# First phase of an adaLN, attention and feed-forward kernel: one PSUM tile for the one-column products, one reading engine per PSUM tile, one more head computed in this phase, weight sums one per step

## The chip, the cores and the metric

The kernel runs on one core of one Trainium2 chip. The metric is the device time of one execution in microseconds (us). The profile's span, from the first to the last instruction, is about 1.7 us shorter than that time. Engines: PE is TensorE (matmuls), DVE is VectorE, ACT is ScalarE, SP only issues DMAs here. The record shows different chips for the later sets of runs (0, 1 and 14), so times are compared with the runs of before in the same set; profiles of different sets are compared across chips.

## The reference, cut to what matters

```python
mod = (silu(c) @ w_mod)            # six vectors of 1024: sa, ca, ga, sb, cb, gb
h = layernorm(x) * (1 + ca) + sa   # x: 2048 x 1024
q = h @ wq                         # 32 heads of 128; K and V: the last 512 rows of the caches
x = x + ga * (softmax(q k^T / sqrt(128)) v @ wo)
h = layernorm(x) * (1 + cb) + sb
x = x + gb * ((silu(h @ w_gate) * (h @ w_up)) @ w_down)
```

The kernel treats x in four chunks of 512 rows. In the first phase it makes the first chunk's normalized and transposed input and the q of the first heads while the weights are still coming in. As sa is known late, q is first computed from `hs = layernorm(x) * (1 + ca)`, and `sa @ wq` is added afterwards as a bias, one column per head (`bias_q`). Then come 128 steps (4 chunks x 32 heads) of scores, exponentials, q of the head seven steps ahead, the products with V, and output projections; then the feed-forward part.

Names in the profiles: xn are normalized rows, hT the transposed (and later modulated) input, wm and wq tiles of w_mod and wq, qT a head's q, s_ps the scores, pT their exponentials, o_ps the products with V, a_ps the output projection, guT the input of the last feed-forward product.

## The kernel before

The parts that the change and the argument touch. PSUM tiles of tag "mm" have four buffers of 512 FP32 columns each (called one bank below), those of tag "s" two buffers of two banks each.

```python
def mm(name, shape=(P, 512), dt=FP32):
    return psp.tile(list(shape), dt, name=name, tag="mm", bufs=4)
def big(name, shape=(P, 2, 512), dt=FP32):
    return psp.tile(list(shape), dt, name=name, tag="s", bufs=2)
# ... all DMA loads are issued from SP, in this order:
for tt in range(QT):
    load_x(tt)
for half in range(DH):
    load_wm(1, half); load_wq8(2 * half); load_wq8(2 * half + 1)   # ca; wq of heads 0..7
load_wm(0, 0); load_wm(0, 1)                                       # sa
# kT: 4 DMA transposes; v_sb: 4 loads
load_wq(0, 2)                                                      # wq of heads 8..11
# ...
h_scale(0, h0_ps[0][:, 0, :])               # DVE;  hs = h * (1 + ca), read from PSUM
mod_cols(1, 0, ca1, True, (1,))
h_scale(1, h0_ps[0][:, 1, :], True)         # ACT, the same PSUM tile
mod_cols(1, 0, ca1, True, (2, 3))
h_scale(2, h0_ps[0][:, 2, :])               # DVE
h_scale(3, h0_ps[0][:, 3, :], True)         # ACT
for dt in (0, 2):
    nc.vector.tensor_copy(out=h10[:, dt:dt + 2, :], in_=h0_ps[0][:, dt:dt + 2, :])
nc.scalar.copy(out=h10[:, 4:8, :], in_=h0_ps[1])
# ... q of heads 4..6 (tag "mm"), then 0..3 (tag "s", two heads in one tile)
for g in range(4):
    q0(g, range(4, DT))
sa_cols(0)                                  # 32 one-column matmuls, DVE copies to sa, sa_bf
q0(4, range(4, DT))
# ... modulation of h10 on DVE
shift_cols(0)                               # 28 one-column matmuls: sa @ wq, lower half
q0(5, range(4, DT))
sa_cols(1)
q0(6, range(4, DT))
shift_cols(1)                               # upper half, DVE adds: bias_q
for g in range(4):
    put_q(g, q0_ps[g], bias_q[:, g:g + 1], g % 2 == 1)   # odd heads on ACT
# ... rest of the modulation; put_q of 4..6; head 7 follows in step 0, between the first scores
```

Of the kernel before, what the change touches and what calls it, by code (L numbers as in the profile page):

```python
# [9 lines left out]
ALU = mybir.AluOpType  # L10
AX = mybir.AxisListType
BF16 = mybir.dt.bfloat16
# [576 lines left out]
def fast_path(ctx, tc, flag, A_x, A_k_cache, A_v_cache, A_wq, A_wo, B_x, B_w_gate, B_w_up,  # L589
# [3 lines left out]
    nc = tc.nc  # L593
    P = 128
    _, S, D = A_x.shape
    _, Hkv, Sk, Dh = A_k_cache.shape
    HD = A_wq.shape[1]
    H = HD // Dh
# [5 lines left out]
    NTC = S // TCW  # L604
    QT = TCW // P
    DT = D // P
# [28 lines left out]
    wk = ctx.enter_context(tc.tile_pool(name="work", bufs=2))  # L635
# [13 lines left out]
    def mm(name, shape=(P, 512), dt=FP32):  # L649
        return psp.tile(list(shape), dt, name=name, tag="mm", bufs=4)  # L650
# [19 lines left out]
    def chain(start):  # L670

        last = {}
        for ins in nc.cur_bb.bb.instructions[start:]:
            if ins.engine in last:
                tc.add_manual_dep(
                    ins, last[ins.engine],
                    mybir.DependencyInfo(mybir.DependencyClass.NoSync,
                                         mybir.DependencyReason.DATA), reason="chain")
            last[ins.engine] = ins.name
# [12 lines left out]
    wm_tiles = {}  # L692
# [14 lines left out]
    H0 = 7  # L707
# [14 lines left out]
    h10 = hpool.tile([P, DT, TCW], BF16, name="hT", tag="hT")  # L722
    load_wm(0, 1)
    kT = blkB("kT", [P, Hkv, W])
    for kv in range(Hkv):
        pin(nc.sync.dma_start_transpose(
            out=kT[:, kv, :], in_=A_k_cache[0, kv, k0:k0 + W, :]), "dma")
# [21 lines left out]
    sa, ca1, sb, cb1 = (modT[:, i, :] for i in range(4))  # L749
# [12 lines left out]
    siluc = const.tile([P, DT], BF16, name="siluc")  # L762
# [5 lines left out]
    def mod_cols(vec, half, dst, add_one, tiles=(0, 1, 2, 3)):  # L768
        wm = wm_tiles[(vec, half)]
        ps = mm("mod_ps", (P, 4))  # L770
        for i in tiles:
            for dt in range(DT):
                nc.tensor.matmul(ps[:, i:i + 1], lhsT=wm[:, dt, i * P:(i + 1) * P],  # L773
                                 rhs=siluc[:, dt:dt + 1], start=(dt == 0), stop=(dt == DT - 1))
        i0, i1 = tiles[0], tiles[-1] + 1
        nc.vector.tensor_scalar(out=dst[:, 4 * half + i0:4 * half + i1], in0=ps[:, i0:i1],
                                scalar1=1.0 if add_one else 0.0, scalar2=None, op0=ALU.add)
# [4 lines left out]
    c_bc = const.tile([P, D], BF16, name="c_bc")  # L782
# [40 lines left out]
    def at(k, f, *a):  # L823
        tasks.setdefault(k, []).append((f, a))
# [15 lines left out]
        nc.scalar.activation(out=mv[:, 2:3], in_=mv[:, 2:3], func=ACT.Exp, scale=-0.5)  # L840
        ln[tt] = mv

    def ln_norm(tt, on_act=False):
        mv = ln.pop(tt)
        n = wk.tile([P, D], BF16, name="xn", tag="xn", bufs=3)
        if on_act:
            nc.vector.scalar_tensor_tensor(out=mv[:, 3:4], in0=mv[:, 0:1], scalar=-1.0,
                                           in1=mv[:, 2:3], op0=ALU.mult, op1=ALU.mult)
            nc.scalar.activation(out=n, in_=xt[tt], func=ACT.Identity, bias=mv[:, 3:4],
                                 scale=mv[:, 2:3])  # L850
        else:
            pin(nc.vector.tensor_scalar(out=n, in0=xt[tt], scalar1=mv[:, 0:1],  # L852
                                        scalar2=mv[:, 2:3], op0=ALU.subtract, op1=ALU.mult))
        return n

    xn = {}

    def ln_rows(tt):
        xn[tt] = ln_norm(tt)

    def ln_xpose(key, tt):
        t = tt % QT
# [5 lines left out]
    def ln_affine(key, dt, ps, sc, sh, on_act):  # L868
        if on_act:
            nc.scalar.activation(out=hT[key][:, dt, :], in_=ps, func=ACT.Identity,  # L870
                                 bias=sh[:, dt:dt + 1], scale=sc[:, dt:dt + 1])
        else:
            pin(nc.vector.tensor_scalar(out=hT[key][:, dt, :], in0=ps, scalar1=sc[:, dt:dt + 1],
                                        scalar2=sh[:, dt:dt + 1], op0=ALU.mult, op1=ALU.add))

    def ln_mod(key, dt, sc, sh):
        ln_affine(key, dt, hT[key][:, dt, :], sc, sh, False)
# [27 lines left out]
    def plan_late_ln(k, key, sc, sh):  # L905

        for t in range(QT):
            tt = key[1] * QT + t
            at(k + 2 * t, late_stats, tt)
            at(k + 10 + 2 * t, ln_rows, tt)  # L910
            at(k + 11 + 2 * t, ln_xpose, key, tt)
        at(k + 8, late_rstd)
        for dt in range(DT):
            at(k + 24 + dt, ln_mod, key, dt, sc, sh)
# [13 lines left out]
    LEAD = H0  # L928
    qT = {}

    def put_q(g, q_ps, bias=None, on_act=False):
        t = wk.tile([P, TCW], BF16, name="qT", tag="row", bufs=LEAD + 2)
        if bias is None:
            nc.vector.tensor_copy(out=t, in_=q_ps)  # L934
        elif on_act:
            nc.scalar.activation(out=t, in_=q_ps, func=ACT.Identity, bias=bias)  # L936
        else:
            nc.vector.tensor_scalar(out=t, in0=q_ps, scalar1=bias, scalar2=None, op0=ALU.add)
        qT[g] = t
# [4 lines left out]
    h0_ps = [big("h0_ps", (P, 4, TCW), BF16) for _ in range(2)]  # L944
# [45 lines left out]
    hs = [blkA("hs", [P, 4, TCW]) for _ in range(DH)]  # L990

    def h_scale(dt, src=None, on_act=False):
        src = h10[:, dt, :] if src is None else src
        if on_act:
            nc.scalar.activation(out=hs[dt // 4][:, dt % 4, :], in_=src, func=ACT.Identity,  # L995
                                 scale=ca1[:, dt:dt + 1])
        else:
            nc.vector.tensor_scalar(out=hs[dt // 4][:, dt % 4, :], in0=src,
                                    scalar1=ca1[:, dt:dt + 1], scalar2=None, op0=ALU.mult)

    h_scale(0, h0_ps[0][:, 0, :])
    mod_cols(1, 0, ca1, True, (1,))
    h_scale(1, h0_ps[0][:, 1, :], True)
    mod_cols(1, 0, ca1, True, (2, 3))
    h_scale(2, h0_ps[0][:, 2, :])
    h_scale(3, h0_ps[0][:, 3, :], True)
    for dt in (0, 2):
        nc.vector.tensor_copy(out=h10[:, dt:dt + 2, :], in_=h0_ps[0][:, dt:dt + 2, :])
    nc.scalar.copy(out=h10[:, 4:8, :], in_=h0_ps[1])

    q0_mm = [mm("q_ps") for _ in range(H0 - 4)]
    q0_ps = {4 + i: t for i, t in enumerate(q0_mm)}

    def w0(g, dt):
        return wq8[dt // 2][:, dt % 2, g * P:(g + 1) * P]

    def q0(g, dts):
        for dt in dts:
            nc.tensor.matmul(q0_ps[g], lhsT=w0(g, dt), rhs=hs[dt // 4][:, dt % 4, :],  # L1019
                             start=(dt == 0), stop=(dt == DT - 1))  # L1020

    sa_bf = const.tile([P, DT], BF16, name="sa_bf")
    bias_q = const.tile([P, H0], FP32, name="bias_q")

    def shift_cols(half):
        ps = mm("sh_ps", (P, H0))
        for g in range(H0):
            for i in range(4):
                dt = 4 * half + i
                nc.tensor.matmul(ps[:, g:g + 1], lhsT=w0(g, dt), rhs=sa_bf[:, dt:dt + 1],  # L1030
                                 start=(i == 0), stop=(i == 3))
        if half == 0:
            nc.vector.tensor_copy(out=bias_q, in_=ps)
        else:
            nc.vector.tensor_tensor(out=bias_q, in0=ps, in1=bias_q, op=ALU.add)  # L1035

    def sa_cols(half):
        mod_cols(0, half, sa, False)
        nc.vector.tensor_copy(out=sa_bf[:, 4 * half:4 * half + 4],
                              in_=sa[:, 4 * half:4 * half + 4])  # L1040

    for dt in range(4):
        for g in range(4, H0):
# [1 line left out]
    for i in range(2):  # L1045
# [4 lines left out]
        if i == 0:  # L1050
            mod_cols(1, 1, ca1, True)
            for dt in range(4, DT):
                h_scale(dt)
    for g in range(4):
        q0(g, range(4, DT))
    sa_cols(0)
    q0(4, range(4, DT))
    for dt in range(4):
        ln_mod(("h1", 0), dt, ca1, sa)
    shift_cols(0)  # L1060
    q0(5, range(4, DT))
    sa_cols(1)
    q0(6, range(4, DT))
    shift_cols(1)
    for g in range(4):
        put_q(g, q0_ps[g], bias_q[:, g:g + 1], g % 2 == 1)
    for dt in range(4, DT):
        ln_mod(("h1", 0), dt, ca1, sa)
    for g in range(4, H0):
        put_q(g, q0_ps[g], bias_q[:, g:g + 1])  # L1070
    chain(first)

    k_ld = []
# [183 lines left out]
    for hg in range(H // 4):  # L1257
        for i in range(2):
            for j in range(2):
                at((1 + hg % (NTC - 1)) * H + max(0, 4 * hg - 3 + 2 * i + j), bound_wq, hg, i, j)  # L1260
    at(NU - H + 2, load_k)
    for kv in range(Hkv):
        at(NU - H + 20 + 2 * kv, bound_k, kv)
# [76 lines left out]
    for k in range(NU + 1):  # L1340
        if k % 4 >= 2 and 4 * (k // 4) + 12 < NU:
            g = 4 * (k // 4) + 12
            load_wq(g // H, (g % H) // 4, (k % 4 - 2,))
        if k < NU:
            emit_s(k)
        if k + LEAD < NU:
            emit_q(k + LEAD)
        if k == NU - 5:
            load_gu(0, 0)
        run_tasks(k)  # L1350
        if k >= 1:
            emit_o(k - 1)
# [76 lines left out]
```

## Time and profile before

| | before |
|---|---|
| time, median of 3 | 1273.99 us (1273.82 to 1274.0) |
| span of the profiled run | 1272.5 us |
| PE / DVE / ACT busy | 99% / 48% / 26% |
| first wide q matmul starts | 12.21 us |
| first o_ps group (product with V) starts | 35.11 us |
| stretch between these two | 22.90 us |

From the first o_ps group on, PE repeats a fixed pattern, so the stretch between the last two marks says how well the first phase runs. The page's busy line:

```profile
PE 1254.6 (99%) x7445; PEld 640.9 (50%) x7587; DVE 608.9 (48%) x1335; ACT 335.3 (26%) x440; POOL 1.3 (0%) x10
```

The timeline of PE in the kernel before, cut to the lines around its idle times. The columns are start, duration, engine, line, operation, output and inputs, shape and count; in brackets the idle time before the group and what ended it.

```profile
12.21 2.82 PE L1019 MATMUL q_ps<-hs,wq 128*128 128x512 bf16 x11
15.49 1.90 PE L1019 MATMUL q_ps<-hs,wq 128*128 128x512 bf16 x8 [0.47 <-DVE hT L1008]
...
29.20 1.02 PE L1148 MATMUL q_ps<-hT,wq 128*128 128x512 bf16 x4 [0.26 <-DVE bias_q L1035]
30.77 0.59 PE L1159 MATMUL s_ps<-qT,kT 128*128 128x512 bf16 x2 [0.54 <-ACT qT L936]
...
32.92 0.59 PE L1148 MATMUL q_ps<-hT,wq 128*128 128x512 bf16 x2
...
35.11 1.07 PE L1191 MATMUL o_ps<-v_sb,pT 128*128 128x130 bf16 x16
```

Wide matmuls follow each other every 0.216 us, and a group's printed duration includes the last one's tail. So the twelve q matmuls from 12.21 (one record of them is missing) need 2.6 us, and PE could have gone on at 14.8 or 14.9; it went on at 15.49. Counted in this way the three idle times are 0.6, 0.4 and 0.7 us. Head 7's eight matmuls are the four at 29.20 and two pairs, cut here, at 31.20 and 32.06.

Where the first of these comes from is seen in the timeline of ACT and DVE over the same microseconds:

```profile
12.19 0.69 ACT L995 ACTIVATE hs<-h_ps,modT 128x512 bf16<-128x512 bf16 x1 [2.06 <-DVE modT L776]
...
12.91 0.48 DVE L998 TENSOR_SCALAR hs<-h_ps,modT 128x512 bf16<-128x512 bf16 x1 [0.36 <-ACT hs L995]
...
13.43 0.69 ACT L995 ACTIVATE hs<-h_ps,modT 128x512 bf16<-128x512 bf16 x1 [0.55 <-DVE hs L998]
...
14.01 1.86 ACT L1009 COPY hT<-h_ps 128x2048 bf16<-128x2048 bf16 x1
14.15 1.29 DVE L1008 COPY hT<-h_ps 128x1024 bf16<-128x1024 bf16 x2 [0.75 <-ACT hs L995]
```

The two engines take turns on one PSUM tile, each waiting for the other. Only the ACT copy at 14.01 overlaps DVE, and it reads the other tile.

One more stall lies in step 32. The groups of o_ps are 5.22 us apart in this part. The timelines of PE and DVE near 180 us:

```profile
178.04 1.07 PE L1191 MATMUL o_ps<-v_sb,pT 128*128 128x130 bf16 x16
...
178.87 1.22 DVE L1082 SCALAR_TENSOR_TENSOR junk<-wq 128x1024 bf16<-128x1024 bf16 x1
...
180.12 1.23 DVE L1082 SCALAR_TENSOR_TENSOR junk<-wq 128x1024 bf16<-128x1024 bf16 x1
...
181.47 1.22 DVE L1082 SCALAR_TENSOR_TENSOR junk<-wq 128x1024 bf16<-128x1024 bf16 x1
...
182.95 1.22 DVE L1082 SCALAR_TENSOR_TENSOR junk<-wq 128x1024 bf16<-128x1024 bf16 x1
...
188.79 1.07 PE L1191 MATMUL o_ps<-v_sb,pT 128*128 128x130 bf16 x16
```

Four weight sums (they feed a bound on the scores) stand in one step, and two steps take 10.75 us instead of 10.45. All waits of PE in the list of waits (total, times, longest) are these:

```profile
PE h_ps L948 <- DVE xn L852: 2.3, 2, 2.1
PE warm_ps L746 <- DVE warm_w L737: 1.6, 1, 1.6
PE s_ps L1159 <- ACT qT L936: 0.5, 1, 0.5
PE q_ps L1019 <- DVE hT L1008: 0.5, 1, 0.5
PE gu_ps L1305 <- DVE guT L1311: 0.3, 1, 0.3
PE q_ps L1148 <- DVE bias_q L1035: 0.3, 1, 0.3
```

### The profile page before, as it was taken

What the parts mean: (1) busy time and instruction counts of PE and PEld (TensorE: products, weight loads), DVE (VectorE), ACT (ScalarE), POOL (GpSimd) and SP (SyncE); (2) the same over time, 40 slices, a digit from 0 to 9 for tenths busy, and PEclk for the clock granted to TensorE, in tenths of its full rate; (3) what the DMA queues carried; (4) which work ended last, traced back from release to release, by engine and by line L of the source; (5) the groups of instructions that cost most, each with busy time, mean ns of one, the idle gap of its engine ahead of it and who ended that gap; (6) DMA issues with size and microseconds to landing.
All of it is one profiled execution on the core that took longest, in us unless ns stands there. A gap on an engine that the chain in (4) does not pass through costs nothing.

```text
span 1272.5 us, 18029 instructions
## 1 busy us (share of the span) xinstructions
PE 1254.6 (99%) x7445; PEld 640.9 (50%) x7587; DVE 608.9 (48%) x1335; ACT 335.3 (26%) x440; POOL 1.3 (0%) x10
## 2 busy tenths in 40 slices
PE   8999999999999999999999999999999999999998
PEld 4555555555555555555554444444444444444444
DVE  4766568966587756476664632321122112221122
ACT  3643334443343333334341111011100111011100
POOL 0000000000000000000000000000000000000000
PEclk9999999999999999999999999999999999999999
DMA  9897658787656655454575479326633565425702
GB/s 291 197 246 182 178 128 174 174 172 193 144 137 171 154 137 153 113 154 115 117 202 146 132 224 252 95 92 209 211 113 111 167 207 188 157 91 168 246 17 69
DMA packets 306844, 204.46 MB, mean 161 GB/s; under 512 B 145601, under 2 KB 303297, under 8 KB 306754
## 3 DMA queue, kind: packets, MB, share of 16 engines
q1 hardware_dynamic: 301842, 199.03, 57.5%
q10 hardware_dynamic: 4912, 4.20, 1.0%
q8 instruction: 61, 1.00, 0.3%
q14 instruction: 29, 0.24, 0.1%
HBM read 165.94 MB, written 4.21 MB: 134 GB/s over the span
## 4 chain that ended last, share of the span: by engine, by line
PE 96%; DVE 1%; DMA 1%; issue 1%; ACT 0%; SPq 0%; DVEq 0%; ACTq 0%
PE gu_ps L1305 29%; PE a_ps L1223 17%; PE q_ps L1148 16%; PE d_ps L1325 15%; PE o_ps L1191 9%; PE s_ps L1159 8%; DMA hT<-xn 1%; PE q_ps L1019 1%; DMA x<-in_A_x_dram 0%; DVE junk L1082 0%; PE mod_ps L773 0%; DVE st L833 0%; DVE xn L852 0%; ACT hs L995 0%; PE sh_ps L1030 0%
## 5 line engine op out<-in xcount | busy, mean ns | idle before, releaser
L1161 ACT ACTIVATE pT<-s_ps 128x1024 bf16<-128x1024 f32 x256 | 249.1, 1020 | 347.0 <-PE s_ps L1159 234.5
L1223 PE MATMUL a_ps<-wo,oT 128*128 128x512 bf16 x989 | 240.1, 379 | 1.9
L1148 PE MATMUL q_ps<-hT,wq 128*128 128x512 bf16 x966 | 228.7, 379 | 0.3 <-DVE bias_q L1035 0.3
L1311 DVE TENSOR_TENSOR guT<-gu_ps,sg 128x512 bf16<-128x512 f32 x112 | 77.4, 691 | 284.1 <-ACT sg L1310 284.1
L1305 PE MATMUL gu_ps<-hT,wg 128*128 128x512 bf16 x875 | 209.8, 379 | 1.4 <-DVE guT L1311 0.3
L1310 ACT ACTIVATE sg<-gu_ps 128x512 bf16<-128x512 f32 x112 | 66.9, 597 | 489.1 <-PE gu_ps L1305 474.9
L1325 PE MATMUL d_ps<-wd,guT 128*128 128x512 bf16 (+2 forms) x934 | 193.2, 366 | 0.9
L1305 PE MATMUL gu_ps<-hT,wu 128*128 128x512 bf16 x659 | 162.0, 379 | 0.7
L1223 PEld LDWEIGHTS <-oT 128*128 128x128 bf16 x1024 | 100.1, 98 | 120.6
L934 DVE CAST qT<-q_ps 128x512 bf16<-128x512 f32 x121 | 83.5, 690 | 148.1 <-PE q_ps L1148 147.1
L1148 PEld LDWEIGHTS <-wq 128*128 128x128 bf16 x968 | 94.7, 98 | 114.2 <-issue 0.3
L1325 PEld LDWEIGHTS <-guT 128*128 128x128 bf16 x952 | 90.9, 98 | 103.0
L1191 PEld LDWEIGHTS <-pT 128*128 128x128 bf16 x2048 | 126.7, 98 | 30.8 <-issue 0.4
L1305 PEld LDWEIGHTS <-wg 128*128 128x128 bf16 x896 | 87.6, 98 | 106.0 <-issue 0.6
L1191 PE MATMUL o_ps<-v_sb,pT 128*128 128x130 bf16 x2048 | 137.1, 220 | 0.1
L1159 PE MATMUL s_ps<-qT,kT 128*128 128x512 bf16 x467 | 129.5, 379 | 2.9 <-ACT qT L936 0.5
L1305 PEld LDWEIGHTS <-wu 128*128 128x128 bf16 x672 | 65.7, 98 | 79.3
L1178 DVE TENSOR_TENSOR oq<-o_ps,rl 128x256 bf16<-128x256 f32 (+2 forms) x256 | 100.3, 418 | 3.7
L1329 DVE TENSOR_TENSOR f<-d_ps,gb_bc 128x512 f32<-128x512 f32 (+2 forms) x34 | 22.4, 660 | 140.8 <-PE d_ps L1325 140.8
L1231 DVE TENSOR_TENSOR acc<-a_ps,acc 128x512 f32<-128x512 f32 x64 | 44.0, 687 | 37.2 <-PE a_ps L1223 37.2
L1159 PEld LDWEIGHTS <-kT 128*128 128x128 bf16 x512 | 44.9, 98 | 31.3 <-issue 1.0
L1305 PE MATMUL gu_ps<-hT,v_sb 128*128 128x512 bf16 x220 | 57.0, 379 | 0.2
(92 smaller groups left out, 419.1 us busy)
## 6 DMA issues: line engine op xcount, KB each, us to landing
wq<-in_A_wq_dram SPq DMA_DIRECT2D x64, 512.0 KB
wo<-in_A_wo_dram SPq DMA_DIRECT2D x64, 512.0 KB
wg<-in_B_w_gate_dram SPq DMA_DIRECT2D x56, 512.0 KB
wd<-in_B_w_down_dram SPq DMA_DIRECT2D x56, 512.0 KB
wu<-in_B_w_up_dram SPq DMA_DIRECT2D x42, 512.0 KB
v_sb<-in_B_w_up_dram SPq DMA_DIRECT2D x14, 512.0 KB
x<-in_A_x_dram SPq DMA_DIRECT2D x16, 256.0 KB
wm<-in_w_mod_dram SPq DMA_DIRECT2D x4, 1024.0 KB
```

Source lines behind the costliest of these rows:

```text
L934: nc.vector.tensor_copy(out=t, in_=q_ps)
L1148: nc.tensor.matmul(q_ps, lhsT=w, rhs=hT[("h1", cc)][:, dt, :], start=(dt == 0), stop=(dt == DT - 1))
L1159: nc.tensor.matmul(s_ps[:, i, :], lhsT=kT[:, kv, j * P:(j + 1) * P], rhs=qT[g], start=True, stop=True)
L1161: nc.scalar.activation(out=p[:, 2 * jj:2 * jj + 2, :], in_=s_ps, func=ACT.Exp, scale=scale)
L1178: nc.vector.tensor_tensor(out=dst, in0=ps[:, s0:s0 + cnt, 0:Dh], in1=sc, op=ALU.mult)
L1191: nc.tensor.matmul(o_slot["ps"][:, s_, :], lhsT=pT[g][:, j, t * P:(t + 1) * P], rhs=v_sb[:, kv, j, 0:VN], start=(j == 0), stop=(j == WT - 1))
L1223: nc.tensor.matmul(a_ps, lhsT=oT[(cc, 2 * q + i)][:, hh % 4, t * P:(t + 1) * P], rhs=wo_tiles[(cc, q, dh, i)][:, hh % 4, :], start=(hh == ...
L1231: nc.vector.tensor_tensor(out=acc[(cc, t)][:, dsl], in0=a_ps, in1=acc[(cc, t)][:, dsl], op=ALU.add)
L1305: nc.tensor.matmul(ps[:, n, :], lhsT=gu_w[(cc, fg, nm, dt // 4)][:, dt % 4, fi * P:(fi + 1) * P], rhs=hT[("h2", cc)][:, dt, :], start=(dt ...
L1310: nc.scalar.activation(out=g, in_=ps[:, 0, :], func=ACT.Silu)
L1311: nc.vector.tensor_tensor(out=guT[(cc, fg)][:, fi, :], in0=ps[:, 1, :], in1=g, op=ALU.mult)
L1325: nc.tensor.matmul(d_ps, lhsT=guT[(cc, f // 4)][:, f % 4, t * P:(t + 1) * P], rhs=wd_tiles[(cc, dh, f // 4)][:, f % 4, c0:c0 + w], start=( ...
```

## The change

Its intent is to remove these idle times. (a) Each PSUM tile has one reading engine: DVE does all four scalings and the copies of h0_ps[0], ACT only copies h0_ps[1]; qT of heads 0 and 1 is written by DVE, of heads 2 and 3 by ACT. (b) The one-column products share one PSUM tile, are cut into pieces, and stand between pairs of wide matmuls. (c) Head 7 is computed in full in the first phase, behind the last one-column products, from the already modulated input h10. (d) The weight sums stand one per step, seven steps ahead of their group's heads; before, the first group's four stood in one step and the others one per step, three steps ahead. (e) The fourth normalized row of the last chunk uses the buffer c_bc, which is free by then.

```diff
-            at(k + 10 + 2 * t, ln_rows, tt)
+            at(k + 10 + 2 * t, ln_rows, tt, c_bc if t == QT - 1 else None)
...
     h_scale(0, h0_ps[0][:, 0, :])
+    nc.scalar.copy(out=h10[:, 4:8, :], in_=h0_ps[1])
     mod_cols(1, 0, ca1, True, (1,))
-    h_scale(1, h0_ps[0][:, 1, :], True)
+    h_scale(1, h0_ps[0][:, 1, :])
...
-    h_scale(3, h0_ps[0][:, 3, :], True)
+    h_scale(3, h0_ps[0][:, 3, :])
...
+    one_ps = mm("one_ps", (P, 3, 8))
...
-    for g in range(4):
+    for g in range(3):
         q0(g, range(4, DT))
-    sa_cols(0)
-    q0(4, range(4, DT))
+
+    q0(3, (4, 5))
+    sa_mm(0, (0, 1))
+    q0(3, (6, 7))
+    sa_mm(0, (2, 3))
+    sa_out(0)
+    q0(4, (4, 5))
+    sh_mm(0, range(4))
+    q0(4, (6, 7))
+    sh_mm(0, range(4, H0))
... # the same for the upper half, with heads 5 and 6
+    for dt in (4, 5):
+        ln_mod(("h1", 0), dt, ca1, sa)
+    for dt in (6, 7):
+        ln_affine(("h1", 0), dt, h10[:, dt, :], ca1, sa, True)
+    nc.vector.tensor_tensor(out=bias_q, in0=one_ps[:, 2, 0:H0], in1=bias_q, op=ALU.add)
+    q0_ps[H0] = mm("q_ps")
+    q0(H0, range(DT), h10)
     for g in range(4):
-        put_q(g, q0_ps[g], bias_q[:, g:g + 1], g % 2 == 1)
+        put_q(g, q0_ps[g], bias_q[:, g:g + 1], g >= 2)
...
-                at((1 + hg % (NTC - 1)) * H + max(0, 4 * hg - 3 + 2 * i + j), bound_wq, hg, i, j)
+                at((1 + hg % (NTC - 1)) * H + 4 * hg - LEAD + 2 * i + j, bound_wq, hg, i, j)
...
-        if k + LEAD < NU:
+        if 0 < k < NU - LEAD:
             emit_q(k + LEAD)
```

Here `sa_mm` makes column sums of sa, `sa_out` has DVE copy them to sa and sa_bf, and `sh_mm` multiplies sa_bf with wq. The last hunk: q of head 8 now follows directly after the first scores.

More of the change, by code (lines that the diff above doesn't have):

```diff
@@ L841, in ln_stats, with ln_norm @@
         ln[tt] = mv
-    def ln_norm(tt, on_act=False):
+    def ln_norm(tt, on_act=False, n=None):
         mv = ln.pop(tt)
-        n = wk.tile([P, D], BF16, name="xn", tag="xn", bufs=3)
+        n = wk.tile([P, D], BF16, name="xn", tag="xn", bufs=3) if n is None else n
         if on_act:
@@ L856, in fast_path, with ln_rows @@
     xn = {}
-    def ln_rows(tt):
-        xn[tt] = ln_norm(tt)
+    def ln_rows(tt, n=None):
+        xn[tt] = ln_norm(tt, n=n)
     def ln_xpose(key, tt):
@@ L1001, in fast_path, with q0 @@
     h_scale(0, h0_ps[0][:, 0, :])
+    nc.scalar.copy(out=h10[:, 4:8, :], in_=h0_ps[1])
     mod_cols(1, 0, ca1, True, (1,))
-    h_scale(1, h0_ps[0][:, 1, :], True)
+    h_scale(1, h0_ps[0][:, 1, :])
     mod_cols(1, 0, ca1, True, (2, 3))
     h_scale(2, h0_ps[0][:, 2, :])
-    h_scale(3, h0_ps[0][:, 3, :], True)
+    h_scale(3, h0_ps[0][:, 3, :])
     for dt in (0, 2):
         nc.vector.tensor_copy(out=h10[:, dt:dt + 2, :], in_=h0_ps[0][:, dt:dt + 2, :])
-    nc.scalar.copy(out=h10[:, 4:8, :], in_=h0_ps[1])
     q0_mm = [mm("q_ps") for _ in range(H0 - 4)]
     q0_ps = {4 + i: t for i, t in enumerate(q0_mm)}
+    one_ps = mm("one_ps", (P, 3, 8))
     def w0(g, dt):
         return wq8[dt // 2][:, dt % 2, g * P:(g + 1) * P]
-    def q0(g, dts):
+    def q0(g, dts, src=None):
         for dt in dts:
-            nc.tensor.matmul(q0_ps[g], lhsT=w0(g, dt), rhs=hs[dt // 4][:, dt % 4, :],
+            nc.tensor.matmul(q0_ps[g], lhsT=w0(g, dt),
+                             rhs=hs[dt // 4][:, dt % 4, :] if src is None else src[:, dt, :],
                              start=(dt == 0), stop=(dt == DT - 1))
@@ L1023, in fast_path, with sh_mm, sa_mm, sa_out @@
     bias_q = const.tile([P, H0], FP32, name="bias_q")
-    def shift_cols(half):
-        ps = mm("sh_ps", (P, H0))
-        for g in range(H0):
+    def sh_mm(half, heads):
+        for g in heads:
             for i in range(4):
                 dt = 4 * half + i
-                nc.tensor.matmul(ps[:, g:g + 1], lhsT=w0(g, dt), rhs=sa_bf[:, dt:dt + 1],
-                                 start=(i == 0), stop=(i == 3))
-        if half == 0:
-            nc.vector.tensor_copy(out=bias_q, in_=ps)
-        else:
-            nc.vector.tensor_tensor(out=bias_q, in0=ps, in1=bias_q, op=ALU.add)
-    def sa_cols(half):
-        mod_cols(0, half, sa, False)
-        nc.vector.tensor_copy(out=sa_bf[:, 4 * half:4 * half + 4],
-                              in_=sa[:, 4 * half:4 * half + 4])
+                nc.tensor.matmul(one_ps[:, 1 + half, g:g + 1], lhsT=w0(g, dt),
+                                 rhs=sa_bf[:, dt:dt + 1], start=(i == 0), stop=(i == 3))
+    def sa_mm(half, tiles):
+        for i in tiles:
+            c = 4 * half + i
+            for dt in range(DT):
+                nc.tensor.matmul(one_ps[:, 0, c:c + 1],
+                                 lhsT=wm_tiles[(0, half)][:, dt, i * P:(i + 1) * P],
+                                 rhs=siluc[:, dt:dt + 1], start=(dt == 0), stop=(dt == DT - 1))
+    def sa_out(half):
+        c = slice(4 * half, 4 * half + 4)
+        nc.vector.tensor_copy(out=sa[:, c], in_=one_ps[:, 0, c])
+        nc.vector.tensor_copy(out=sa_bf[:, c], in_=sa[:, c])
     for dt in range(4):
@@ L1053, in fast_path @@
                 h_scale(dt)
-    for g in range(4):
+    for g in range(3):
         q0(g, range(4, DT))
-    sa_cols(0)
-    q0(4, range(4, DT))
+    q0(3, (4, 5))
[7 more added lines that the diff above has]
+    sh_mm(0, range(4, H0))
     for dt in range(4):
         ln_mod(("h1", 0), dt, ca1, sa)
-    shift_cols(0)
-    q0(5, range(4, DT))
-    sa_cols(1)
-    q0(6, range(4, DT))
-    shift_cols(1)
+    nc.vector.tensor_copy(out=bias_q, in_=one_ps[:, 1, 0:H0])
+    q0(5, (4, 5))
+    sa_mm(1, (0, 1))
+    q0(5, (6, 7))
+    sa_mm(1, (2, 3))
+    sa_out(1)
+    q0(6, (4, 5))
+    sh_mm(1, range(H0))
+    q0(6, (6, 7))
+    for dt in (4, 5):
[5 more added lines that the diff above has]
+    q0(H0, range(DT), h10)
     for g in range(4):
-        put_q(g, q0_ps[g], bias_q[:, g:g + 1], g % 2 == 1)
-    for dt in range(4, DT):
-        ln_mod(("h1", 0), dt, ca1, sa)
+        put_q(g, q0_ps[g], bias_q[:, g:g + 1], g >= 2)
     for g in range(4, H0):
         put_q(g, q0_ps[g], bias_q[:, g:g + 1])
+    put_q(H0, q0_ps[H0])
     chain(first)
```

## The prediction

> **What bounds the kernel now.** TensorE (PE): the page's busy table gives it 1254.6 of 1272.5 us (99%); VectorE (DVE) 48%, ScalarE (ACT) 26%. The PE timeline shows 512-column matmuls every 0.216 us. The change keeps every matmul, so it can only remove PE idle time. Taking starts in the PE timeline against the count of matmuls times 0.216 us (32 single columns: 0.78), the idle time within reach is:
>
> - a, 14.9 to 15.5 us: 0.6. Heads 0 and 1 need the PSUM tile h0_ps, whose readers alternate between DVE and ACT until 15.44 (timeline). The Trainium skill, "PSUM — Partial Sum Buffer", section on bank collisions, says two engines may not access one bank at once, two reads included; the trace agrees: these reads never overlap.
> - b, 28.8 to 29.2: 0.4, head 7 waits for bias_q (DVE).
> - c, 30.06 to 30.77: 0.7, the first scores wait for ACT's qT, which waited for DVE's qT of the same PSUM tile.
> - d, step 32, near 184 us: four weight sums of 1.22 us stand in one step on DVE. Groups of o_ps start 5.22 us apart; here two steps take 10.75: 0.3.
> - e, 770 us: the list of waits shows PE waiting 0.3 for guT; before it DVE waited 4.67 for the buffer of the fourth xn.
>
> Sum: 2.3 us. The start-up to 12.2 us stays.
>
> **What the change does.**
> - a: four scalings (0.48 each) and both copies (0.65 each) all go to DVE; ACT reads only the other tile. DVE ends near 14.9: gains 0.55.
> - b, c: head 7 (8 matmuls, 1.73 us) runs while DVE adds bias_q and both engines write qT from separate tiles: gains about 1.1.
> - New costs: only two q matmuls (0.43) stand between the column sums of sa and their use, while DVE needs 0.62 to sa_bf (before: 23.99 to 24.61): two new PE waits of 0.2. With five q matmuls of filler gone, the scores of head 1 wait about 0.25 for ACT's exponentials (0.94 each). More switches between narrow and wide matmuls: 0.1.
> - First phase net: about 0.95 gained.
> - d: one sum per step, gains 0.3. Sums now meet statistics (some 5.5 to 6.4 us of DVE work in 5.22), but the pile, 3.3 us late, cost only 0.3: no cost.
> - e: c_bc serves as fourth xn: gains 0.3.
>
> **Prediction.** 1273.99 - 1.55 = 1272.4 us; 8 in 10 between 1271.2 and 1273.5. Faster by over 2%: 0.005; within 2%: 0.99; slower: 0.005. PE is the chain: all gains are on the critical path, 0.12% of it.
>
> **What would show it.** PE timeline: the second group of q matmuls starts near 14.9, not 15.49; the first o_ps group near 34.15, not 35.11; no wait of scores for ACT qT, none of q for bias_q; new small PE waits on sa_bf (DVE) and pT (ACT). Near 184 us no two steps of 10.75; no wait on guT at 770. PE's busy time unchanged, span 1.5 us less.
>
> **What would make it wrong.** The weight tile of head 8 lands late: its loads fill the DMA until 32.3 us (windows), and head 8 now starts about 31.1 instead of 33.8; then the first-phase gain shrinks by up to 1 us. bias_q stands behind four modulations on DVE; if these run late, the second sa product waits. If moved sums make DVE late at steps 37 to 40 or 49 to 52, new PE waits appear there.

## The result, and the profile after

| | before | changed |
|---|---|---|
| median of 6 | 1273.9 us | 1274.15 us |
| range | 1273.74 to 1274.39 | 1273.31 to 1275.05 |
| span of the profiled run | 1272.5 | 1272.4 |
| first wide q matmul | 12.21 | 11.32 |
| first o_ps group | 35.11 | 35.42 |
| stretch | 22.90 | 24.10 |
| from 665 us (the last o_ps group of 16) to the end | 607.39 | 606.95 |

The ratio of the times is 1.0001, with a 95% interval of 0.9988 to 1.0014. Such ratios are the mean time of one kernel's fast runs over that of the other's fast runs of the same rounds, so they are not quite the ratio of the medians quoted. The change brought nothing, where a gain of 1.55 us had been forecast, and the measured time lies outside the range of 1271.2 to 1273.5.

The timeline of PE in the changed kernel, cut to what answers the lines shown of before:

```profile
11.32 4.57 PE L1020 MATMUL q_ps<-hs,wq 128*128 128x512 bf16 x19
15.73 0.94 PE L773 MATMUL mod_ps<-siluc,wm 128*128 128x1 bf16 x32
16.54 2.32 PE L1020 MATMUL q_ps<-hs,wq 128*128 128x512 bf16 x9
19.39 2.76 PE L1020 MATMUL q_ps<-hs,wq 128*128 128x512 bf16 x12 [0.54 <-DMA wq<-in_A_wq_dram]
22.39 0.55 PE L1038 MATMUL one_ps<-siluc,wm 128*128 128x1 bf16 x16 [0.24 <-DMA wm<-in_w_mod_dram]
...
30.48 1.03 PE L1182 MATMUL s_ps<-qT,kT 128*128 128x512 bf16 x4
32.30 0.82 PE L1171 MATMUL q_ps<-hT,wq 128*128 128x512 bf16 x3 [0.79 <-DMA wq<-in_A_wq_dram]
32.95 0.59 PE L1182 MATMUL s_ps<-qT,kT 128*128 128x512 bf16 x2
33.39 0.38 PE L1171 MATMUL q_ps<-hT,wq 128*128 128x512 bf16 x1
34.12 0.39 PE L1171 MATMUL q_ps<-hT,wq 128*128 128x512 bf16 x1 [0.35 <-DMA wq<-in_A_wq_dram]
...
35.42 1.07 PE L1214 MATMUL o_ps<-v_sb,pT 128*128 128x130 bf16 x16
```

All three waits that the change aimed at are gone: the first twenty q matmuls form one row (one record missing; 4.41 us where 20 x 0.216 is 4.32), nothing waits for bias_q, and no scores wait for ACT's qT. In their place stand four waits for DMA. Counted with 0.216 us per wide matmul they are 0.69, 0.41, 0.96 and 0.51 us, together 2.57 us. PE started 0.89 us earlier in this execution, because the rows of x had come earlier (DVE's last wait for them ended at 5.13 instead of 6.16), and still ended the phase 0.31 us later. That ACT and DVE may now work at the same time is seen at 11.43 us, where ACT copies its tile while DVE reads the other:

```profile
11.24 0.48 DVE L998 TENSOR_SCALAR hs<-h_ps,modT 128x512 bf16<-128x512 bf16 x1
...
11.43 1.86 ACT L1002 COPY hT<-h_ps 128x2048 bf16<-128x2048 bf16 x1 [2.28 <-PE mod_ps L773]
```

The Trainium skill, "PSUM — Partial Sum Buffer", section "PSUM bank collisions raise a hardware error", on which the prediction drew, says that two engines may not access one PSUM bank at the same time, two reads included. No read shown here goes against that, but it does not account for all of the turns in the kernel before. A tile of tag "s" is two banks. DVE's first copy at 14.15 reads the first bank of h0_ps[0] and still waited 0.75 us for ACT's last scaling, which reads the second; ACT's qT of head 1 waited for DVE's of head 0 (until 29.95), though each head's q fills a bank of its own. There the turns went by tile. Whether tiles of one bank each would have removed these two waits without moving work was not tested.

The chain that ended last, followed back from the end, now leaves PE at 34 us and goes down the DMA queue. Its pieces in order of time (start, duration, what), changed kernel:

```profile
28.07 0.51 SPq L664
...
28.62 5.45 DMA wq<-in_A_wq_dram
...
34.12 0.39 PE q_ps L1171
```

In the kernel before, this chain stays on PE, DVE and ACT from the transposes at 10.04 us to the end of the first phase. SP's own timeline (SPq rows are the issuing of DMAs, which goes in order) shows why the weights come so late:

```profile
14.83 10.23 SPq L726 DMA_TRANSPOSE kT<-in_A_k_cache_dram  x4
25.11 2.92 SPq L664 DMA_DIRECT2D v_sb<-in_A_v_cache_dram  x4
28.07 1.55 SPq L664 DMA_DIRECT2D wq<-in_A_wq_dram  x2
```

The weights of heads 8 to 11 stand behind K and V, and are issued only at 28.07 us. The Trainium skill, "Perfetto Trace Analysis", section "DMA Instruction — HWDGE (DVE, Sync)", says that the profiled window of such an instruction is the issuing alone and not the movement of the data. This trace agrees: issuing ended at 29.62, and PE waited for the two tiles until 32.30 and 34.12. The loads also ended later than in the kernel before: from 32.5 to 33.5 us DMA still moved 233 and 136 GB/s (two half microseconds), before 27 and 0. Why is not shown; the second profile of the changed kernel has 280 and 153, that of before 182 and 23.

The second loss is in the steps. The pile at step 32 is gone (two steps take 10.45 us there), but a new stall of the same size stands where the sums of the third group now are. PE and DVE near 220 us in the changed kernel:

```profile
220.14 1.07 PE L1214 MATMUL o_ps<-v_sb,pT 128*128 128x130 bf16 x16
...
220.44 1.21 DVE L804 SCALAR_TENSOR_TENSOR junk<-wmT,c_bc 128x1024 bf16<-128x1024 bf16 x1
...
221.59 0.69 DVE L1258 TENSOR_TENSOR f<-a_ps,acc 128x512 f32<-128x512 f32 x1
...
222.19 1.22 DVE L1105 SCALAR_TENSOR_TENSOR junk<-wq 128x1024 bf16<-128x1024 bf16 x1
...
223.33 1.28 DVE L833 BATCH_NORM_STATS2 st<-x 128x6 f32<-128x512 bf16 x2
...
224.53 0.67 DVE L1259 TENSOR_TENSOR f<-f,ga_bc 128x512 f32<-128x512 f32 x1
...
225.28 0.66 DVE L1261 TENSOR_TENSOR x<-f,x 128x512 bf16<-128x512 f32 x1
```

The next whole group of 16 starts at 236.14: three steps took 16.00 us, where 3 x 5.22 = 15.67. A step here holds a product with c_bc (1.21), a weight sum (1.22), statistics (1.28) and three operations of a last projection (2.0 in all) besides its q copy and its outputs.

### The profile page after: what moved, and what is told of

It reads as the page before. It is cut to its first block, busy times and chain, and to the rows that moved or that the text cites. A ratio compares the mean times of both kernels' runs of the same rounds, so it can differ in the third digit from the quotient of the medians.

```text
span 1272.4 us, 18018 instructions
## 1 busy us (share of the span) xinstructions
PE 1255.9 (99%) x7445; PEld 640.0 (50%) x7587; DVE 610.0 (48%) x1335; ACT 335.6 (26%) x440; POOL 1.3 (0%) x10
## 4 chain that ended last, share of the span: by engine, by line
PE 95%; SPq 2%; DVE 1%; issue 1%; DMA 0%
PE gu_ps L1328 30%; PE a_ps L1246 17%; PE q_ps L1171 16%; PE d_ps L1348 15%; PE o_ps L1214 9%; PE s_ps L1182 8%; SPq L664 1%; SPq L726 1%; DMA wq<-in_A_wq_dram 0%; DVE junk L1105 0%; DVE st L833 0%; DVE junk L804 0%; DVE oq L1201 0%; DVE qT L934 0%; DVE f L1259 0%
```

## The experiments

Theory 1: the first phase is bounded by the arrival of data, and the kernel before ran just behind it. The waits that were removed had been hiding waits for DMA. Rival: the new order itself costs the time, by the new waits for sa_bf and for the exponentials and by less filler between the first scores. Theory 2: the early sums, not something else, cause the stall near 220 us.

The first four kernels shared the runs of before (1274.36 us median, 1273.27 to 1274.42, 9 runs).

### e1_wq_early

```diff
+    load_wq(0, 2)
     kT = blkB("kT", [P, Hkv, W])
     ... # four transposes, V
-    load_wq(0, 2)
```

> The changed kernel, with the two loads of the weights of heads 8 to 11 put ahead of the four K transposes and the V loads in the DMA queue. Theory 1 (the first phase of the changed kernel ends when these weights land, so what PE gained was handed to a wait for DMA): PE's waits for this tile (0.79 and 0.35 us in the changed kernel) go, the first o_ps group starts near 34.2 us instead of 35.42, and the time is 0.8 to 1.4 us below the changed kernel. Rival (the new order itself costs it: waits on sa_bf, on the exponentials, less filler between the first scores): the first o_ps group stays within 0.3 us of 35.4, and the time is the same.

Measured: 1273.16 us median (1272.67 to 1273.23, 5 runs), ratio 0.9990 (0.9976 to 1.0003). Its timeline, cut to four lines of PE and SP:

```profile
12.61 4.60 PE L1020 MATMUL q_ps<-hs,wq 128*128 128x512 bf16 x19
...
14.96 5.17 SPq L664 DMA_DIRECT2D wq<-in_A_wq_dram  x2
...
20.17 7.50 SPq L727 DMA_TRANSPOSE kT<-in_A_k_cache_dram  x4
...
34.37 1.07 PE L1214 MATMUL o_ps<-v_sb,pT 128*128 128x130 bf16 x16
```

The list of PE's waits names no DMA any more, and the stretch is 34.37 - 12.61 = 21.76 us, 1.14 us shorter than before's 22.90 and 2.34 shorter than the changed kernel's. The 2.34 include the changed kernel's early start: against its second profile below (start 12.73, stretch 22.78) e1 is 1.02 us shorter at nearly the same start. The same PE, DVE and ACT work in the same order, only with these weights coming earlier and K and V later, gives the gain that the prediction had forecast for the first phase (0.95). The rival falls. The time is 0.99 us below the changed kernel's median, as expected, though from another set of runs; the interval against before holds 1, but all five runs lie below all nine of before, by 0.04 us at the closest. The edit moves the issue of these loads from 28.07 to 14.96 us. That an earlier issue brings an earlier start of the transfer fits what the Trainium skill, "DMA: Bandwidth & Descriptors", section "Two DMAs through the same engine are not ordered", states: within one queue of one DMA engine, descriptors start in order (it adds that nothing orders transfers across the engines). That PE did not wait for the tiles agrees with it.

### e2_before_wq_early

The same edit in the kernel before.

> The kernel before, with the same loads put ahead of K and V. Its PE waited for no DMA after 12 us, so theory 1 expects no gain: within 0.2 us of before, first o_ps group at 35.1 plus or minus 0.3. If the load order is a gain by itself, it would be about 1 us faster, and the change would have no part in it.

Measured: 1273.72 us median (1273.25 to 1274.72, 5 runs), ratio 0.9997 (0.9983 to 1.0010); stretch from 12.25 to 35.16, 22.91 us. So the load order alone leaves the first phase as it was. The median is 0.6 us below before's, more than the 0.2 expected, but the runs overlap, and the profiles' first phases are alike.

### e3_sums_mix

The changed kernel, with only the first group's sums early:

```diff
-    4 * hg - LEAD + 2 * i + j, bound_wq, hg, i, j)
+    4 * hg - (LEAD if hg == 0 else 3) + 2 * i + j, bound_wq, hg, i, j)
```

> The changed kernel, but only the first group of weight sums stands early (steps 25 to 28); the others stand where the kernel before had them. Theory 2 (the early sums of group 3 at steps 37 to 40 meet statistics and the last additions of a_ps on DVE, and cost PE 0.33 us near 220 us): no pair of o_ps groups is further apart than the count of steps times 5.22 us, neither near 184 nor near 220 us, and the time is 0.3 us below the changed kernel. If the stall near 220 us has another cause, it stays.

Measured: 1273.67 us median (1273.24 to 1274.94, 5 runs), ratio 0.9997 (0.9983 to 1.0010). No steps are out of line any more, neither near 184 nor near 220 us: from the first to the last whole o_ps group of the steps it takes 629.69 us, where before takes 630.00 and the changed kernel 630.03. Theory 2 holds, and the 0.3 us of the prediction's part d exist, but only with this placement. The first phase ended as in the changed kernel (11.73 to 35.26, with a wait of 1.50 us for the weights of head 8 in the list). The total time is too noisy for 0.3 us; the steps' spacing shows it.

### e4_both

Both edits on the changed kernel.

> The changed kernel with both: weights ahead of K and V, and only the first group of sums early. If theories 1 and 2 hold, the gains add: 1.1 to 1.7 us below the changed kernel, about 1272.6 us, first o_ps group near 34.2 us and no stall near 184 or 220 us.

Measured: 1272.62 us median (1272.27 to 1272.91, 5 runs), ratio 0.9987 (0.9973 to 1.0000). All five runs lie below all nine of before, and the median is 1.53 us below the changed kernel's (from another set), within the range expected. The stretch is 12.39 to 34.49, 22.10 us; no stalls in the steps. It has a wait for the weights of sa (0.17 us listed, 0.32 counted), which e1, starting 0.22 us later, did not have.

The next four shared another set of runs of before (1273.67 us median, 1273.56 to 1275.57, 9 runs).

### e5_mixed_readers

e4_both, with ACT doing `h_scale(1)` and `h_scale(3)` again and its copy last.

> The kernel e4_both with part a undone: DVE and ACT again take turns at reading the PSUM tile h0_ps. Theory (each part of the change in the first phase is worth what the wait before it showed, once DMA no longer ends the phase): the PE wait on DVE's copies comes back, 0.5 us, and the stretch from the first wide q matmul to the first o_ps group is 22.6 us instead of 22.1. Rival (PE still ends the phase at the arrival of weights): the stretch does not grow.

Measured: 1273.08 us median (1272.68 to 1273.15, 5 runs), ratio 0.9993 (0.9979 to 1.0006). The wait for DVE's copies came back as expected, 0.47 us in the list. But the stretch (11.89 to 34.23) grew to 22.34, by 0.24 us instead of 0.5: the wait of e4_both for the weights of sa is absent here. In e4_both PE reached these weights 9.99 us after its first wide q matmul (by count) and waited until 10.31; here it reached them after 10.57 us and did not wait. Neither side was right alone: in these two executions half of part a is a gain, and half is taken by the next arrival.

### e6_qT_alternate

e4_both, with `g % 2 == 1` for ACT again.

> The kernel e4_both with DVE and ACT again reading the same PSUM tile for heads 0 and 1, and for 2 and 3. In the kernel before, this made the first scores wait 0.7 us; here head 7's eight matmuls (1.73 us) stand in between. If that filler hides it, the stretch from first q to first o_ps stays within 0.2 us of 22.1; if the split of readers is what removed the wait, it grows by 0.5 to 0.7 us.

Measured: 1272.83 us median (1271.9 to 1272.95, 5 runs), ratio 0.9989 (0.9976 to 1.0003). The stretch is 12.07 to 34.43, 22.36 us, 0.26 more than e4_both, a little over the 0.2 allowed. The list of waits has none for qT, and from the first scores to the first o_ps group it takes 3.70 us against 3.69. The difference lies in waits for DMA: the 22 wide matmuls from 17.30 would end by count at 22.05 and the next group starts at 22.64, so 0.59 us idle. Of these, 0.18 lie inside the row, where the tenth matmul was followed only at 19.63 by the next, for a tile of the first heads' wq, and 0.41 after it, for sa's weights; e4_both has 0.32, all for sa's weights. So head 7 as filler hides the shared reading of qT, and the split by tile is not needed for it.

### e7_before_d_e

The kernel before, with the sums placed as in e3 and with c_bc as the fourth buffer.

> The kernel before, with the first phase untouched, the first group of weight sums early and c_bc as the fourth buffer of xn. The pair of o_ps groups near 178 us is 10.45 apart, not 10.75. After 665 us the kernel takes 606.95 us: a wait of 0.3 us near 770 us that before's profile had was absent in e2, which had the old buffers, so e is worth 0.3 in some executions only. Time 0.3 to 0.6 us below before.

Measured: 1273.46 us median (1273.24 to 1273.65, 5 runs), ratio 0.9996 (0.9982 to 1.0010): 0.2 us below before, less than expected. In the profile both parts are there: no pair of steps of 10.75, 606.96 us after the last whole group. The stretch is 12.05 to 34.95, 22.90 us: before's first phase, unchanged.

### e8_three_between

e4_both, with the one-column sums in one piece and three wide matmuls between them and their use (cut):

```diff
+    sa_mm(0, range(4))
+    sa_out(0)
+    q0(4, (4, 5, 6))
+    sh_mm(0, range(H0))
... # two modulations, bias_q, two modulations
+    q0(4, (7,))
+    q0(5, (4, 5))
+    sa_mm(1, range(4))
+    sa_out(1)
+    q0(5, (6, 7))
+    q0(6, (4,))
+    sh_mm(1, range(H0))
+    q0(6, (5, 6, 7))
```

> The kernel e4_both, with three wide q matmuls (0.65 us) instead of two (0.43) between the last column sum of sa and its use, and the column sums in one piece. DVE needs 0.62 us from the last sum to sa_bf, so both PE waits of 0.17 us on sa_bf should go: the stretch from first q to first o_ps is 0.3 us shorter than in e4_both, about 21.7 us. If the small gaps there are the cost of switching between narrow and wide matmuls, nothing changes.

Measured: 1272.5 us median (1271.94 to 1272.83, 5 runs), ratio 0.9989 (0.9975 to 1.0002); all five runs below all nine of before. PE no longer waits for sa_bf. Yet the stretch (11.57 to 33.57) is 22.00 us, not 21.7. The list of waits of the weight-load side of PE says what took the rest:

```profile
PEld L1038 <- DMA wm<-in_w_mod_dram: 0.8, 2, 0.5
PEld L1178 <- DMA kT<-in_A_k_cache_dram: 0.5, 1, 0.5
...
PEld L1020 <- DMA wq<-in_A_wq_dram: 0.5, 1, 0.5
```

Loading a matmul's weights runs ahead of the matmuls (for head 8 in the kernel before, 32.71 against 32.92 us), so these waits reach PE in part: by count, matmuls could have gone on at 18.95, 24.93 and 29.66 us and started at 19.10, 25.13 and 29.86, so 0.14, 0.20 and 0.20 us. The first is for a tile of the first heads' wq, the second for the weights of sa (the other wait for them did not reach PE), the last for K, for which PE waited in no earlier profile. In this execution each gain on PE meets the next arrival.

### The three single looks

> The kernel before once more, for a second profile. If theory 1 holds in general and not only in the one execution profiled: no PE wait for DMA between the first wide q matmul and the first o_ps group, and this stretch is 22.9 us again. The wait near 770 us for guT may be there or not: it was in one of two profiles of kernels with the old buffers.

Before again: 1273.84 us. PE started at 11.66, 0.55 us earlier than in the first profile, and the first o_ps group came at 35.06, only 0.05 earlier: the stretch is 23.40, not 22.9, and there is a wait for DMA, against the expectation. The timeline of PE in this run:

```profile
32.78 0.61 PE L1148 MATMUL q_ps<-hT,wq 128*128 128x512 bf16 x2 [0.24 <-DMA wq<-in_A_wq_dram]
```

Its weight-load side waited for these weights twice:

```profile
PEld L1148 <- DMA wq<-in_A_wq_dram: 1.2, 2, 0.7
```

The same weights of head 8. Counted, PE lost 0.41 us to the first tile and 0.10 to the second (until 34.19), which is the whole difference between 23.40 and 22.90. So even the kernel before was held by them in this execution, in which x came early. That supports theory 1 in a stronger form than it was stated.

> The changed kernel once more, for a second profile. Theory 1: PE waits for the weights of head 8 again, by 0.7 us or more in all, and the first o_ps group starts at 35.3 plus or minus 0.4 us wherever the first wide q matmul starts. The stall of 0.33 us near 220 us is there again. If the waits for DMA were a chance of one execution, they are absent and the first o_ps group starts near 34.3.

The changed kernel again: 1274.42 us. PE started at 12.73, 1.41 us later than in the first profile, and the first o_ps group came at 35.51, 0.09 later. It waited for the weights of head 8 twice (0.69 and 0.23 us in the timeline). Three steps near 220 us take 16.00 us again.

> The kernel e4_both with part e undone: the fourth xn waits for a transpose to free a buffer again. DVE waits for that transpose 3 to 5 us near 765 us; PE waits for guT near 770 us by 0 to 0.3 us. After 665 us it takes 606.9 us without that wait and 607.2 with it.

e4_both with the old buffer for xn: 1272.57 us. DVE waited 2.92 us for the transpose, a little less than expected, and PE did not wait for guT; 606.8 us after the last whole group.

The waits in the last column are counted from the matmuls' 0.216 us, as above; the list of waits shows less, since it measures from the printed end of a group.

| profile | first wide q | first o_ps | stretch | waits of PE for DMA, counted |
|---|---|---|---|---|
| before | 12.21 | 35.11 | 22.90 | none |
| before again | 11.66 | 35.06 | 23.40 | 0.51 |
| changed | 11.32 | 35.42 | 24.10 | 2.57 |
| changed again | 12.73 | 35.51 | 22.78 | 1.24 |
| e1, weights early | 12.61 | 34.37 | 21.76 | none |
| e4, and sums placed anew | 12.39 | 34.49 | 22.10 | 0.32 |
| e8, and three between | 11.57 | 33.57 | 22.00 | 0.54 |

The changed kernel's two profiles start 1.4 us apart and end the phase 0.1 us apart, and e3, with the same first phase, starts at 11.73 and ends at 35.26: in these three its end does not depend on when PE begins, but on when the weights land. A stretch is therefore in part a measure of the start. With the weights early, e1, e4, e5, e6 and e11 start between 11.89 and 12.61 and end between 34.21 and 34.49, and e5, which has part a undone, ends before e4. So differences of 0.2 to 0.3 us between single profiles, as in e5 and e6, do not show what a part is worth in time; which wait is there, they do show.

## Why the prediction was wrong

- "First phase net: about 0.95 gained": the step that failed. The mechanism and nearly the size were right for PE, DVE and ACT (1.14 us between e1 and before; of the new costs, head 1's scores lost 0.05 us in e1 by count, where 0.25 for the exponentials had been set down), but the sum had no term for data. The prediction worked out that head 8 would be asked for at 31.1 instead of 33.8 us while its loads filled the DMA until 32.3, wrote this down as what would make it wrong, and still counted the gain in full. Its figures left too much room besides: the kernel before had asked for head 8 at 32.92, not 33.8, and in the changed kernel, which asked at 31.34 by count, PE got the two tiles only at 32.30 and 34.12 in the first profile. What stood in the place of the gain were 2.57 us of waits for DMA, and even the earlier start was lost in them; the second profile has 1.24 us of them, so "up to 1 us" was nearly right for that one.
- "All gains are on the critical path": wrong. PE being busy or waiting for DVE before does not show that DVE is the only bound there; before again, with PE half a microsecond earlier, waited for DMA. How late data would have to be asked for was not in the list of waits, since what is there in time is not listed.
- Parts a, b and c: the waits on h0_ps, bias_q and ACT's qT went as described. In e6 the last of these is gone with head 7 as filler alone.
- "Two new PE waits of 0.2" on sa_bf: right (0.18 and 0.16 us counted in the changed kernel), and e8 removed them.
- "d: one sum per step, gains 0.3 ... no cost": wrong. The pile's 0.30 went and 0.33 came at 220 us. The three additions of the last projection on DVE (2.0 us) had not been counted. With the other groups left in place (e3) the 0.3 is kept. The prediction named steps 37 to 40 as a risk; the stall is there.
- "e: gains 0.3": not in general. Of the four profiles with the old buffer (before, before again, e2, e11), DVE waited 2.9 to 4.7 us in each, but PE waited in one only.
- Range: a forecast of 1.55 us, on a kernel whose runs spread over 0.65 us before and 1.7 us after, deserved a range that held "no gain".

What stays open: why DVE's last wait for rows of x ends between about 5.1 and 6.7 us (PE starts its q matmuls between 11.3 and 12.7), which goes with a spread of the times that was not traced run by run; why the loads ended later in the changed kernel; and how fast the first phase can be with the best order of all loads. e4_both and e8_three_between have the lowest medians, about 0.1% below before (ratios 0.9987 and 0.9989), which the rounds' intervals (to 1.0000 and 1.0002) do not separate from 1. What speaks for a gain is the separation of all single runs, which e1, e5 and e6 have too, and the profiles.

## What to carry to other kernels

Before a wait of the busiest engine is counted as a gain, find out when the data of the next few operations land, and compare that with when the change will ask for them: a wait on another engine can hide an arrival that is less than a microsecond behind it. Then move the loads together with the work: here neither the load order alone (ratio 0.9997) nor the change alone (1.0001) was worth anything that the runs separate from nothing, and together they shortened the first phase by 1.14 us and put all five runs below all nine of before (0.9990, interval to 1.0003). When work is moved out of a pile on a side engine, add up all that stands in the new steps, not only the average.

## What the Trainium skill lacked or had wrong

- "Perfetto Trace Analysis", section "DMA Instruction — HWDGE (DVE, Sync)": it says which part of a DMA the profile shows, but gives no duration for the issuing when many loads are under way. Here issuing four K transposes took SP 10.23 us behind the earlier loads, and four loads of V after them 2.92 us; what stood behind them in the queue was issued 13 us later than when the transposes began (14.83 to 28.07).
- "PSUM — Partial Sum Buffer", section "PSUM bank collisions raise a hardware error": it says that two readers of one bank must be kept apart, not what taking turns costs, nor that a program may order readers by whole tiles. Here turns, one of them between different banks of a tile (0.75 us on DVE), held a tile until 15.44 and PE for 0.6 us.
- No page drawn on here says that a list of waits hides arrivals that are just in time; the two profiles of the kernel before, with none and 0.24 us of listed waits of PE for DMA at starts of 12.21 and 11.66 us, show it.
